# A column-tiled memory update, a second queue for the first input block, and a new set of scheduling priorities in a gated mix of memory attention and a gated feed-forward layer

## The chip, the cores and the metric

The kernel runs on one core of a Trainium2 chip. The metric is the device time of one execution in microseconds (us). All runs in this document are in the fast state: this is a program for one core, and no run was over 1.5% above the fastest of the same kernel. TensorE, VectorE, ScalarE and GpSimd are written PE, DVE, ACT and POOL in the profile; PEld is TensorE's weight load, and SP is the engine that issues most transfers.

## The reference

The output is `g*a + (1-g)*b`, where `a` is attention in four segments of 512 positions with a running memory, and `b` is a gated GELU layer. The part that matters here is the memory: after each segment `M` and `z` are updated from `phi(k)` and `v`, and the next segment reads them.

```python
x = A_x                                   # (1, 2048, 512) bf16; 32 heads of 16; N = 4 segments of L = 512
g = sigmoid((x * gate_w).sum(-1, keepdims=True))
phi = lambda t: where(t > 0, t + 1.0, exp(t))
for s in range(N):                        # q, k, v = x@wq, x@wk, x@wv, split by heads and segments
    p = softmax(qs @ ks.T * scale + mask)         # mask: causal inside the segment
    a_dot = p @ vs
    a_mem = (phi(qs) @ M) / (phi(qs) @ z + 1e-6)
    outs.append(gb * a_mem + (1 - gb) * a_dot)    # gb = sigmoid(beta), per head
    M = M + phi(ks).T @ vs                # the memory update: a 16 x 16 block per head
    z = z + phi(ks).sum(over positions)
a = concat(outs) @ wo
b = (gelu(x @ w_gate) * (x @ w_up)) @ w_down      # width 1792
# ... (reshapes, casts and the input generator are cut)
```

## The kernel before

The program is a graph of tasks. A list scheduler in the host code places them: at each step it takes the task that can start first by its estimates, and of several the one with the highest priority. A priority is the longest estimated path to the end plus a hand-tuned bias per task name. Thus the order of the instructions on every engine follows from the tasks, their estimates and the biases together.

```python
BIAS = {"D0": -56, "D1": -233, "D2": -96, ..., "mz0": -1, "mz1": -9, "mz2": -35, "mzacc0": 7, ...}   # some 130 entries
...
t.prio = min(t.est.values()) + best + t.bias      # best: the highest priority among the successors
...
k = (st, -t.prio - (OPEN_BONUS if open_ else 0.0), t.id)   # st: when the engine, the inputs and a PSUM bank are free
```

The memory update (tasks `mz`) of a segment multiplies `phi(k)`, four chunks `t` of 128 features (8 heads each), with the values of those heads and a column of ones, over four blocks `kt` of 128 positions. A matmul makes a 128 x 136 block, of which only the eight 16 x 17 blocks on the diagonal are wanted. VectorE adds the whole block to an accumulator (`mzacc`) and masks it (`mzbd`).

```python
for i in range(2):
    gm = Grp(banks)                       # one PSUM bank
    pieces(f"mz{s}_{i}", gm, [
        mm(gm, lambda gm=gm, t=t, i=i: gm.f32()[:, 136 * (t - 2 * i):136 * (t - 2 * i) + 136],
           phkt[:, kt, t * 128:(t + 1) * 128],
           Vaug[sl][:, kt, :, 4 * t:4 * t + 4, :].rearrange("p j i c -> p i j c"),
           [("phkt", t), ("Vaug", sl, kt)], kt == 0, kt == 3, 136)
        for t in (2 * i, 2 * i + 1) for kt in range(4)], 4)
    ...
    task(f"mzacc{s}_{i}", DVE, [first], grp=gm)          # copy or add of 272 columns
    task(f"mzbd{s}_{i}", DVE, [Instr(lambda e, i=i: e.tensor_tensor(
        MZbd[:, 2 * i:2 * i + 2, :], MZacc[:, 2 * i:2 * i + 2, :],
        bdmask[:, :].rearrange("p (o c) -> p o c", o=1).to_broadcast([P, 2, 136]), ALU.mult), ...)])
```

The product of probabilities and values (tasks `pv`, "PV" below) already works in column-tile mode: four matmuls, each with 17 weight columns in its own quarter of the array (`tile_position=(0, 32*q)`), run side by side: a group of four with 64 columns starts every 29 ns in the kernel before. The scores work in row-tile mode (32 contraction rows each). All else uses the full array.

At the start, the first block of x comes in two halves from the SP queue, then the weights. Sixteen transposes turn it, two into each of eight PSUM areas, and eight copies of 256 columns take it out. Six full-array matmuls on zeros run before that.

```python
for a in range(2):
    dma(f"x0_{a}", SP, lambda a=a: xin[:, 2 * a:2 * a + 2, :], ...)
for c0, c1 in ((0, 128), (128, 512)):
    for key, w, src in (("wk", wk, A_wk), ("wq", wq, A_wq)):
        wdma((key, c0 > 0), SP, ...)
...
for i in range(6):
    gw = Grp(banks)
    task(f"warm{i}", PE, [Instr(lambda e, gw=gw: e.matmul(gw.f32()[:, :], warm[:, 0:128], warm, ...)])
for u in range(2):                        # half of x
    for kb in range(4):                   # block of 128 features
        ...                               # two transposes into one area, one copy of 256 columns (ACT or DVE)
```

The softmax here doesn't subtract the row's maximum and nothing guards it: scores larger than these inputs give would overflow.

## Time and profile before

| What | Value |
|---|---|
| Time, median of the three runs there were | 272.45 us (272.41 to 272.8) |
| Span of the profiled execution | 270.3 us |
| DVE, ACT, POOL busy | 69%, 78%, 36% of the span |
| DMA, mean over the span | 61 GB/s |

The prediction below shows the page's lines on TensorE, so here are only two views that it tells in words. The first is the timeline of TensorE in the kernel before, at the start. A row has the start in us from the start of the span, the time until the last of the group ends, the engine, the source line, the operation, output and input, weight and moving sizes, the number of instructions, and in brackets how long the engine stood idle before it and what ended that.

```profile
3.80 1.06 PE L533 MATMUL psXALL<-ident,hT 128*128 128x128 bf16 x8
4.65 0.91 PE L533 MATMUL psW<-ident,hT 128*128 128x128 bf16 x8
5.71 1.02 PE L439 MATMUL psW<-xT,wk 128*128 128x512 bf16 x4
7.18 2.76 PE L439 MATMUL psW<-xT,wk 128*128 128x512 bf16 x12 [0.45 <-DMA wk<-in_A_wk_dram]
```

The sixteen transposes run into one another, the first K projection follows, and the other three wait 0.45 us for the second part of wk. The second view is the groups of the kernel before by instruction shape: busy time and mean ns after the first bar, idle time before them after the second.

```profile
L439 PE MATMUL psW<-vaug,phkt 128*128 128x136 bf16 x48 | 3.5, 224 | 0.0
L758 DVE TENSOR_TENSOR mzbd<-mzacc,bdmask 128x272 bf16<-128x272 f32 x6 | 2.5, 464 | 0.0
```

These are the 48 memory-update matmuls and the six masked products. 224 ns is the length of one record, not what a matmul costs: one starts every 63 ns, as the prediction works out.

### The profile page before, as it was taken

To read this page: it belongs to the slowest core of one execution; us is meant where nothing else is said; L and a number is where in the kernel's file an instruction comes from. 1 tells how busy PE (TensorE), PEld (TensorE's weight loads), DVE (VectorE), ACT (ScalarE), POOL (GpSimd) and SP (SyncE) were. 2 spreads that over 40 slices of the span, in tenths; PEclk is the share of its full clock that TensorE was granted. 3 is DMA by queue.
4 is the path that set the end of the run, shared out by engine and by line. 5 is a ranking of instruction groups with operands and counts; after the bars stand their busy time and mean duration, and the time that the engine had idled before them with its cause. 6 is when DMAs were issued, how large, how long until landed. Compare 5 with 4: busy or idle time off the path is not lost.

```text
span 270.3 us, 6945 instructions
## 1 busy us (share of the span) xinstructions
PE 260.6 (96%) x2928; PEld 122.1 (45%) x2969; DVE 186.9 (69%) x333; ACT 211.4 (78%) x180; POOL 96.5 (36%) x223
## 2 busy tenths in 40 slices
PE   7999999999999999999999999999999999999996
PEld 4444434345544353534444444534444444444454
DVE  2779888987889867878608969897642668443451
ACT  4998799989898897979778988986867767776602
POOL 8327785331003864432104723262200253352300
PEclk9999999999999999999999999999999999999999
DMA  6997992000213410032200320112020000000002
GB/s 192 208 308 157 372 230 24 0 4 2 41 39 65 104 49 23 2 78 41 44 0 0 41 42 19 41 23 62 19 44 0 1 2 2 19 22 23 18 2 78
DMA packets 32023, 16.52 MB, mean 61 GB/s; under 512 B 21368, under 2 KB 31992, under 8 KB 31992
## 3 DMA queue, kind: packets, MB, share of 16 engines
q1 hardware_dynamic: 31992, 16.07, 25.8%
q8 instruction: 23, 0.38, 0.6%
q14 instruction: 8, 0.07, 0.1%
HBM read 8.14 MB, written 2.10 MB: 38 GB/s over the span
## 4 chain that ended last, share of the span: by engine, by line
PE 89%; DVE 3%; ACT 3%; issue 2%; DMA 2%; SPq 1%; ACTq 0%
PE psW L439 72%; PE psXALL L774 8%; PE psW L823 5%; DMA wk<-in_A_wk_dram 2%; PE psXALL L439 1%; PE psW L831 1%; DVE oT L858 1%; ACT klow L638 1%; ACT pt L781 1%; ACT hT L908 1%; SPq L470 1%; DVE kpad_1 L661 0%; ACT L908 0%; DVE otok L725 0%; ACT pex L618 0%
## 5 line engine op out<-in xcount | busy, mean ns | idle before, releaser
L781 ACT ACTIVATE pt<-psXALL 128x2048 bf16<-128x2048 f32 x64 | 120.0, 1875 | 27.6 <-PE psXALL L774 22.9
L785 POOL TENSOR_SCALAR_AFFINE_SELECT pt<-pt 128x256 bf16<-128x256 bf16 x128 | 56.9, 446 | 142.8 <-ACT pt L781 121.1
L929 DVE TENSOR_TENSOR hT<-psW,hT 128x512 bf16<-128x512 f32 x56 | 37.8, 686 | 26.0 <-PE psW L439 25.6
L439 PE MATMUL psW<-xT,wu 128*128 128x512 bf16 x215 | 51.4, 380 | 1.3 <-issue 1.1
L439 PE MATMUL psW<-xT,wg 128*128 128x512 bf16 x214 | 49.7, 379 | 1.3 <-issue 1.0
L439 PE MATMUL psW<-wd,hT 128*128 128x512 bf16 x202 | 49.4, 380 | 0.9 <-issue 0.6
L838 DVE STREAM_TRANSPOSE tb<-psW 128x512 f32<-128x512 f32 x32 | 21.0, 696 | 19.1 <-PE psW L831 19.1
L439 PEld LDWEIGHTS psW<-xT,wg 128*128 128x128 bf16 x224 | 20.6, 98 | 25.3 <-issue 1.9
L439 PEld LDWEIGHTS psW<-xT,wu 128*128 128x128 bf16 x224 | 20.2, 98 | 24.5 <-issue 2.1
L439 PEld LDWEIGHTS psW<-wd,hT 128*128 128x128 bf16 x210 | 18.9, 98 | 22.9 <-issue 2.7
L908 ACT ACTIVATE hT<-psW 128x512 bf16<-128x512 f32 x28 | 16.5, 597 | 7.6 <-PE psW L439 7.6
L785 POOL TENSOR_SCALAR_AFFINE_SELECT ptl<-ptl 128x2048 bf16<-128x2048 bf16 x8 | 17.0, 2120 | 12.2 <-ACT ptl L781 10.2
L823 PE MATMUL psW<-pt,vaug 128*17 128x192 bf16 (+3 forms) x512 | 18.7, 273 | 0.0
L781 ACT ACTIVATE ptl<-psXALL 128x2048 bf16<-128x2048 f32 x8 | 15.0, 1877 | 4.6 <-PE psXALL L774 4.5
L439 PE MATMUL psW<-xT,wk 128*128 128x512 bf16 x60 | 15.2, 380 | 1.2 <-issue 0.6
L439 PE MATMUL psW<-xT,wq 128*128 128x512 bf16 x61 | 15.8, 379 | 0.3 <-issue 0.2
L693 POOL COPY exsT<-exs 32x4 f32<-32x4 f32 x64 | 14.5, 226 | 3.7
L439 PE MATMUL psW<-wo,oT 128*128 128x512 bf16 x56 | 14.9, 379 | 0.5 <-issue 0.5
L439 PE MATMUL psW<-wv,xT 128*128 128x512 bf16 x61 | 14.8, 380 | 0.3 <-issue 0.2
L981 DVE TENSOR_SCALAR ost<-psW,omgt 128x512 bf16<-128x512 f32 x8 | 6.0, 748 | 13.1 <-PE psW L439 13.1
L823 PEld LDWEIGHTS psW<-pt,vaug 128*17 128x17 bf16 x512 | 10.2, 90 | 8.2 <-POOL pt L785 2.1
L456 DVE CAST hT<-psW 128x512 bf16<-128x512 f32 x19 | 12.6, 678 | 0.9 <-PE psW L439 0.8
(104 smaller groups left out, 307.9 us busy)
## 6 DMA issues: line engine op xcount, KB each, us to landing
out_dram<-ost SPq DMA_DIRECT2D x15, 128.0 KB, 1.7
wg<-in_B_w_gate_dram SPq DMA_DIRECT2D x2, 896.0 KB, 6.7
wu<-in_B_w_up_dram SPq DMA_DIRECT2D x2, 896.0 KB, 6.0
wd<-in_B_w_down_dram SPq DMA_DIRECT2D x1, 1792.0 KB, 13.0
vlow<-vaug SPq DMA_DIRECT2D x8, 136.0 KB, 3.4
hT<-in_A_x_dram SPq DMA_DIRECT2D x2, 256.0 KB, 3.0
wv<-in_A_wv_dram SPq DMA_DIRECT2D x1, 512.0 KB, 6.3
wo<-in_A_wo_dram SPq DMA_DIRECT2D x1, 512.0 KB, 13.9
```

Source lines behind the costliest of these rows:

```text
L439: return Instr(lambda e: e.matmul(view(), lhsT, rhs, start=first, stop=last), reads=reads, writes=[fkey if fkey is not None else g.key], e ...
L456: alts[DVE] = [Instr(lambda e: e.tensor_copy(dst(), src()), reads=reads, writes=writes, est=dve_t(n))]
L470: return e.dma_start(out_ap(), in_ap())
L693: cross = task(f"exsT{s}", POOL, [Instr(lambda e, g=g, c=c: e.tensor_copy(exsT[sl][32 * g:32 * g + 32, c:16:4], exs[32 * c:32 * c + 32, s4 ...
L774: instrs.append(Instr(lambda e, g=g, lhs=lhs, rhs=rhs, c0=c0, ncol=ncol: e.matmul(X[g][:, c0:c0 + ncol], lhs(32 * g), rhs(32 * g), start=T ...
L781: prev_exp[0] = exp_task(s, f"exp{s}_{t}{name}", [Instr(lambda e: e.activation(dst[:], XALL[:, :].rearrange("p (g c) -> p g c", g=4), ACTF ...
L785: task(f"msk{s}_{t}{name}", POOL, [Instr(lambda e, view=view, pat=pat, base=base: e.affine_select(out=view, in_=view, compare_op=ALU.is_ge ...
L823: instrs.append(Instr(lambda e, t=t, q=q, kb=kb, slot=slot, c0=c0: e.matmul(gp.f32()[32 * q:32 * q + 17, 128 * kb + 64:512], Vaug[sl][:, k ...
L838: task(f"pvt{s}_{t}_{j}", DVE, [Instr(lambda e: e.transpose(Tb[:, j, :], gp.f32()[:, :]), [gp.key], [("Tb", j)], dve_t(512))], grp=gp)
L908: lambda e, g=g, ft=ft, s=s: e.activation(hT[s % 2][:, ft, :], g.f32()[:, :], ACTF.Gelu_apprx_tanh),
L929: task(f"Um{s}_{ft}", DVE, [Instr(lambda e, g=g, ft=ft: e.tensor_tensor(hT[sl][:, ft, :], g.f32()[:, :], hT[sl][:, ft, :], ALU.mult), [g.k ...
L981: DVE: [Instr(lambda e, view=view, gt=gt, tile=tile: e.tensor_scalar(ostage[tile % N_OST][:], view(), omgt[:, gt:gt + 1], None, ALU.mult), rd,
```

## The change

There are three parts. **Memory update:** each chunk of 128 features is cut in four tiles of 32 (two heads each), which run side by side in column-tile mode (25 to 33 ns for a group of four, as the traces below show), so that a tile makes 32 x 34 values instead of 128 x 136. This makes 64 small matmuls per segment instead of 16, one PSUM bank instead of two, and a quarter of the columns for TensorE to stream. The task carries the scheduler's tag of the PV bursts, so it can be placed inside one. **Start:** the second half of x0 is issued from the ACT queue, and the transposes are evacuated in four copies of 512 columns (two blocks of 128 features at a time, side by side in one PSUM bank) instead of eight of 256. **Priorities:** all biases are new. The code for a gate on VectorE is also added, but `GATE_DVE = ()` leaves it out of the program; that part of the diff is cut here, as are the buffers' declarations and the lines for the transposes.

```diff
 BIAS = {
-    "D0": -56, "D1": -233, "D2": -96, "D3": -332, "G0": -8, ...
+    "D0": -106, "D1": -371, "D2": -43, "G0": -115, ...
     (all entries replaced)
@@ start
-        dma(f"x0_{a}", SP, lambda a=a: xin[:, 2 * a:2 * a + 2, :],
+        dma(f"x0_{a}", (SP, ACT)[a], lambda a=a: xin[:, 2 * a:2 * a + 2, :],
 ...
-            dst = xT[0][:, kb, 256 * u:256 * u + 256]
+            dst = xT[0][:, 2 * i:2 * i + 2, 256 * u:256 * u + 256]
@@ memory update
-            for i in range(2):
-                gm = Grp(banks)
-                pieces(f"mz{s}_{i}", gm, [ ... 16 full-array matmuls, as above ...
+            gm = Grp(banks)
+            m = task(f"mz{s}", PE, [
+                Instr(lambda e, t=t, kt=kt, c=c: e.matmul(
+                    gm.f32()[32 * c:32 * c + 32, 34 * t:34 * t + 34].rearrange("p (j e) -> p j e", e=17),
+                    phkt[:, kt, t * 128 + 32 * c:t * 128 + 32 * c + 32], Vaug[sl][:, kt, :, 4 * t + c, :],
+                    start=(kt == 0), stop=(kt == 3), tile_position=(0, 32 * c)),
+                    [("phkt", t), ("Vaug", sl, kt)], [gm.key], 0.009)
+                for t in range(4) for kt in range(4) for c in range(4)], grp=gm)
+            m.tiled = "pv"
+            m.patience = PATIENCE
 ...
+            task(f"mzbd{s}", DVE, [ ... four products of 32 partitions x 136, instead of two of 128 x 272 ...
```

## The prediction

> **What bounds the kernel now.** I read the page first (parts 1, 2 and 4).
>
> ```profile
> PE 260.6 (96%) x2928; PEld 122.1 (45%) x2969; DVE 186.9 (69%) x333; ACT 211.4 (78%) x180; POOL 96.5 (36%) x223
> PE   7999999999999999999999999999999999999996
> PEclk9999999999999999999999999999999999999999
> PE 89%; DVE 3%; ACT 3%; issue 2%; DMA 2%; SPq 1%; ACTq 0%
> ```
>
> TensorE is busy 96% of 270.3 us at full clock, in every slice but the first and the last, and 89% of the chain that ended last is TensorE. Busy time alone does not prove a bound, because matmul records overlap, so I then read start-to-start times off the timeline of TensorE:
>
> ```profile
> 53.58 0.40 PE L774 MATMUL psXALL<-qT,kpad_0 32*128 32x320 bf16 x8
> 53.90 0.61 PE L823 MATMUL psW<-pt,vaug 128*17 128x448 bf16 x16
> 54.34 0.29 PE L831 MATMUL psW<-ptl,vlow 128*17 128x64 bf16 x16
> 54.46 0.61 PE L823 MATMUL psW<-pt,vaug 128*17 128x448 bf16 x16
> 54.90 0.29 PE L831 MATMUL psW<-ptl,vlow 128*17 128x64 bf16 x16
> 55.34 0.81 PE L439 MATMUL psW<-xT,wg 128*128 128x512 bf16 x3 [0.16 <-issue]
> ...
> 64.89 0.81 PE L439 MATMUL psW<-wv,xT 128*128 128x512 bf16 x3
> 65.53 1.17 PE L439 MATMUL psW<-vaug,phkt 128*128 128x136 bf16 x16
> 66.54 0.59 PE L439 MATMUL psW<-xT,wq 128*128 128x512 bf16 x2
> ```
>
> From these: two 512-column matmuls end 0.59 us after the first starts and one lasts 0.38, so one starts every 0.21 us (0.216 in the single records). Sixteen memory-update matmuls take (1.17 - 0.22)/15 = 63 ns each. In column-tile mode (L823, L831) four matmuls run at a time: the sixteen of L831 start at 54.34 and the next group at 54.46, so a group of four 64-column ones costs (54.46 - 54.34)/4 = 0.03 us (29 ns in single records). I then compared every stretch of the weight-load records, which are complete (2969), with these pitches plus one cost per change of mode. From about 7.2 us on the whole execution leaves only about 3 us unexplained, spread over some 160 stretches, none above 0.3 us. So between 7.2 us and the last matmul (267.7) TensorE is issue-bound without real gaps: what is taken off TensorE's issue time comes off the span, and work of other engines is hidden. The beginning is the one place where it waits:
>
> ```profile
> 2.33 4.80 DMA wk<-in_A_wk_dram
> 7.18 1.05 PE psW L439 x4
> ```
>
> The second K projection starts when the second part of wk lands (7.13 us).
>
> [...] the step from a 512-column matmul to a row-tile one is 0.312 us in place of 0.216, so about 0.095 us; row-tile to column-tile costs about the same (0.171 after a 192-column group that itself needs 0.077). [...] This trace has column tiles only with 17-column weights; the change loads 32, so no record of it tells the cost. [...] (216 ns at 512 columns; the one-column gate matmuls start every 25 ns). [...] the first two x0 issues are 0.51 us apart and land 0.75 us apart (3.70 and 4.45).
>
> **The change part by part.**
>
> Memory update, the main part. Removed: 3 segments x 16 matmuls x 63 ns = 3.02 us of TensorE. Added: 3 x 64 matmuls with 34 columns and 32-column weights, four at a time, 16 groups per segment. [...] I take it to start no faster than the floor of 25 to 29 ns; at 27 ns a segment is 0.43 us, three are 1.30 us. Gain 1.72 us. Modes: the order in which instructions stand in the two built programs shows segments 1 and 2 between score matmuls and a PV burst, which had a change of mode there already. Segment 0 stands between score matmuls and gate matmuls, which costs one more row-to-column change: 164 changes before, 165 after, +0.09 us. Net -1.63 us. All other matmuls are the same in number and shape, so TensorE's remaining issue time is the same.
>
> Evacuation of the memory: VectorE loses six copies or adds (414 to 431 ns) and six masked products (464), about 5.3 us, and gets three additions of 136 columns (about 0.3) and twelve 32-partition products (about 0.25): about 4 us. At 69% busy this is hidden.
>
> Start. The second x0 half is issued at about 0.8 us on ACT instead of 1.33 on SP, and all weight loads move up by 0.5 us. But the trace shows the stretch from about 3 to 7 us as a chain of landings (3.70, 4.45, 5.57, 7.13) for 256, 256, 128 and 384 KB, that is, limited by transfer, not by issue: the same bytes come before wk's second part. Also the 16 transposes start every 0.107 us [...] from 3.80 to 5.5, with no gap at the arrival of the second half, so this half is not awaited now; and if both halves share the engines, the first may land later. Evacuation in four instructions of 512 columns (about 0.6 on ACT, from the 595 ns row of the same size, and 0.43 on VectorE) instead of eight of 256 (0.38 and 0.29) saves perhaps 0.2 us of engine time but starts the last one later. I expect wk's second part 0.0 to 0.5 us earlier and TensorE able to use about half of it: -0.2 us.
>
> New priorities. They reorder nearly all rows: all V projections of segment 0 now come before the first scores, so the first exponentials start some 3.5 us later, and memory update 0 moves from 65 us to near 27. They can remove no TensorE work, and before there was nearly nothing to win from gaps (about 3 us of small change). The risk is one-sided: ACT has 22% idle, but a new place where scores wait for an exponential or PV for its mask would show. I allow +0.2 us. The tail (24 matmuls of 512 and 36 of 256 after the last PV) is the same in both orders.
>
> Sum: 272.45 - 1.63 - 0.2 + 0.2 = 270.8; because some of the small change may go with fewer stretches I say 270.7.
>
> **The rivals.** (a) Weight loads become the limit of the tiled memory update. [...] gain only 0.5 us, time about 271.9. For it: [...] 192 more load and matmul pairs than the 48 removed. Against it: the 17-column groups run at the pace of their streams. One in four. (b) The instructions themselves limit: 128 tiny ones in a row, then 128 of PV. The PV bursts run 128 in 1.1 us without a wait; 32 klow pairs ran in 0.23 us, so bursts are fast, but none this long was tested. It would give about the same loss. One in eight. (c) The new order starves TensorE: 3.5 us of later exponentials come back as a wait at the turn of a segment, where ACT must finish all exponentials before the gelus. It would make 271.5 to 273. One in eight. (d) The start gains in full: 0.5 us or more, time 270.2 or less. One in five. (e) VectorE or a DMA becomes the bound: no, VectorE loses work and the DMA is idle most of the time.
>
> **Range and chances.** Best case: all of the mz gain at 20 ns per group (2.0 us) and 0.6 us at the start and 0.4 of small change: 269.4. Worst likely: weight loads limit and 1 us of new stalls: 272.4. Two per cent is 5.45 us: even deleting the whole memory update, 3.0 us, would not reach it, and a loss of 5.45 us needs gaps that this scheduler did not leave before. So nearly all chance is on the same.
>
> **What would show it.** The memory-update group: 192 matmuls with 64 in about 0.6 us (0.43 plus the 0.2 us a last record lasts); rival (a) or (b) if 64 take over 0.9. The landing of wk's second part and the first start after it: earlier than 7.18 by 0 to 0.5. Idle time of TensorE between 8 us and the end: as small as now; rival (c) if the waits of scores on ACT grow by a microsecond. The prediction is wrong if the span falls by more than 3.0 us (work I have not seen went away, or gaps I took for fixed costs) or rises.

## The result, and the profile after

The changed kernel took 270.35 us in the median (270.18 to 272.21, six runs), the kernel before 272.38 us in the same rounds (271.75 to 272.8, six runs). The ratio of the fast runs is 0.9936 with an interval of 0.9909 to 0.9963, which is "the same" at 2%. A ratio is here always the mean time of one kernel's fast runs over that of the other's of the same rounds, so it is not quite the ratio of the medians quoted. The six times after are 270.18, 270.26, 270.29, 270.40, 270.43 and 272.21; the profile happens to be of the last, which is an outlier that has to be explained on its own.

These are the lines on busy time and on the chain's engines of the page of the changed kernel.

```profile
PE 266.1 (98%) x3113; PEld 121.6 (45%) x3113; DVE 186.0 (69%) x333; ACT 212.1 (78%) x179; POOL 95.2 (35%) x223
PE 97%; DMA 1%; ACT 0%; issue 0%; ACTq 0%
```

There are 144 more weight loads (2969 before), which is 192 less 48, and the chain is now nearly all TensorE: VectorE and ScalarE, 3% each before, are gone from it. The busy time of TensorE is higher than before, but that count is not complete: 41 of 2969 matmul records were missing before (2928) and none after. The weight-load records are complete in both, and all start-to-start times below are from them.

The timeline of TensorE in the changed kernel shows the memory update of segments 0 and 1 in their places (segment 2 is shown with an experiment).

```profile
27.21 0.40 PE L788 MATMUL psXALL<-qT,kpad 32*128 32x448 bf16 x8
27.54 0.72 PE L755 MATMUL psW<-vaug,phkt 128*32 128x34 bf16 x64
28.19 0.60 PE L442 MATMUL psW<-xT,wg 128*128 128x512 bf16 x2
...
100.23 0.71 PE L755 MATMUL psW<-vaug,phkt 128*32 128x34 bf16 x64
100.82 0.62 PE L837 MATMUL psW<-pt,vaug 128*17 128x448 bf16 x16
101.26 0.30 PE L845 MATMUL psW<-ptl,vlow 128*17 128x64 bf16 x16
101.51 0.62 PE L837 MATMUL psW<-pt,vaug 128*17 128x448 bf16 x16
```

The 64 matmuls are one uninterrupted group of about 0.7 us with its tail, where sixteen full ones took 1.17. From the first load of the update to the first load of what follows it is 0.648 us in segment 0, with the change back to full mode in it, 0.564 us in segment 1 and 0.545 us in segment 2. In segment 1, the second PV group starts 0.25 us after the L845 group before it, where the same step is 0.12 in the PV bursts that the prediction shows: it waits for VectorE's addition of the memory update. This view of the changed kernel, the instructions that touch `mzacc`, shows that addition (columns after the count: shortest, median, longest ns; the time of the first and of the last).

```profile
L770 DVE TENSOR_TENSOR mzbd<-mzacc,bdmask x12: 279/290/297, 31.3 to 163.1; 32x136 bf16<-32x136 f32 x12
L767 DVE TENSOR_TENSOR mzacc<-psW,mzacc x2: 299/300/301, 101.1 to 161.7; 128x136 f32<-128x136 f32 x2
```

The addition runs from 101.1 to 101.4, and the PV group follows at 101.51. In segment 2 the same step is 0.11 us, so this is the only place where the new update adds a wait. Now the start, first from the chain of the changed kernel, then from its timeline.

```profile
0.81 3.40 DMA hT<-in_A_x_dram
4.26 1.48 PE psXALL L536 x12
5.75 0.61 ACT xT L543
6.41 12.28 PE psW L442 x48
```

```profile
6.41 5.37 PE L442 MATMUL psW<-xT,wk 128*128 128x512 bf16 x16 [0.26 <-ACT xT L543]
```

Before, the second K projection waited for wk. In this execution the chain goes through x0: its landing, the transposes, one evacuation on ScalarE. All 16 K matmuls then follow without a break, but in this execution they took 5.37 us, and the single records show one start every 427 ns until about 10.1 us, twice the usual 216: TensorE was still at half its usual pace. (This is read from the steps, and the recorded expectations call it the half clock; the granted clock in the profile stands at 1.00 throughout.) This is what makes it the slow one of the six.

### The profile page after: what moved, and what is told of

Same layout as the page of the kernel before. It is cut to its first block, busy times and chain, and to the rows that moved or that the text cites. A ratio compares the mean times of both kernels' runs of the same rounds, so it can differ in the third digit from the quotient of the medians.

```text
span 270.5 us, 7272 instructions
## 1 busy us (share of the span) xinstructions
PE 266.1 (98%) x3113; PEld 121.6 (45%) x3113; DVE 186.0 (69%) x333; ACT 212.1 (78%) x179; POOL 95.2 (35%) x223
## 4 chain that ended last, share of the span: by engine, by line
PE 97%; DMA 1%; ACT 0%; issue 0%; ACTq 0%
PE psW L442 78%; PE psXALL L788 9%; PE psW L837 6%; PE psXALL L442 1%; PE psW L845 1%; DMA hT<-in_A_x_dram 1%; PE psW L755 1%; PE psXALL L536 1%; ACT xT L543 0%; ACT ost L971 0%; ACTq L337 0%
## 5 line engine op out<-in xcount | busy, mean ns | idle before, releaser
L799 POOL TENSOR_SCALAR_AFFINE_SELECT pt<-pt 128x256 bf16<-128x256 bf16 x128 | 55.4, 434 | 139.3 <-ACT pt L795 132.7
L442 PE MATMUL psW<-xT,wu 128*128 128x512 bf16 x224 | 52.7, 380 | 0.0
L442 PE MATMUL psW<-xT,wg 128*128 128x512 bf16 x224 | 52.3, 380 | 0.0
L442 PE MATMUL psW<-wd,hT 128*128 128x512 bf16 x210 | 51.7, 380 | 0.0
L788 PE MATMUL psXALL<-qT,kpad 32*128 32x320 bf16 (+3 forms) x512 | 25.5, 273 | 0.0
L788 PEld LDWEIGHTS psXALL<-qT,kpad 32*128 32x128 bf16 x512 | 7.6, 92 | 26.5 <-ACT pt L795 20.8
L442 PE MATMUL psW<-xT,wk 128*128 128x512 bf16 x64 | 17.2, 412 | 0.3 <-ACT xT L543 0.3
L442 PE MATMUL psW<-wo,oT 128*128 128x512 bf16 x60 | 15.8, 381 | 0.0
L459 DVE CAST hT<-psW 128x512 bf16<-128x512 f32 x21 | 14.1, 680 | 1.7 <-PE psW L442 1.5
```

The lines of the kernel that those rows point to most:

```text
L442: return Instr(lambda e: e.matmul(view(), lhsT, rhs, start=first, stop=last), reads=reads, writes=[fkey if fkey is not None else g.key], e ...
L459: alts[DVE] = [Instr(lambda e: e.tensor_copy(dst(), src()), reads=reads, writes=writes, est=dve_t(n))]
L788: instrs.append(Instr(lambda e, g=g, lhs=lhs, rhs=rhs, c0=c0, ncol=ncol: e.matmul(X[g][:, c0:c0 + ncol], lhs(32 * g), rhs(32 * g), start=T ...
L799: task(f"msk{s}_{t}{name}", POOL, [Instr(lambda e, view=view, pat=pat, base=base: e.affine_select(out=view, in_=view, compare_op=ALU.is_ge ...
```

## The experiments

Eleven kernels were run, in three calls; kernels of one call share the runs of the kernel before, on the same chip. To compare traces without the randomness of the start, I use one length throughout: from the first weight load after the 16 loaded for the K projections to the last weight load of the execution. I call it the body; the time up to it is the start. All traces have some 3.0 us after the last load, but for mz_only with 3.75.

### after_again: the changed kernel once more

Nothing is edited. It gives a profile of a typical execution and the comparison for the other runs of its call.

> The changed kernel once more, unchanged, for a profile of a typical execution. Theory: the profiled execution of 272.21 us was slow because its K projections ran at half clock (427 ns from start to start until 10.1 us); a typical one has 216 ns there, a span near 268.6 us and a time near 270.3 us, 2.0 us less than the kernel before. Rival: the half clock belongs to the change and this profile shows it again, with a time near 272. In either case the memory update takes 0.55 to 0.60 us per segment.

The median is 270.32 us (269.78 to 270.60, five runs) against 272.11 (271.55 to 272.56, 27 runs); ratio 0.9936 [0.9924, 0.9947]. The result repeats. The start in the timeline of TensorE:

```profile
4.17 1.89 PE L536 MATMUL psXALL<-ident,hT 128*128 128x128 bf16 x16 [0.17 <-DMA hT<-in_A_x_dram]
6.32 3.84 PE L442 MATMUL psW<-xT,wk 128*128 128x512 bf16 x16 [0.26 <-ACT xT L543]
```

The K matmuls take 3.84 us here instead of 5.37. The body starts at 9.78 us instead of 11.40, and is 256.10 us long against 256.09: the outlier lost its time before the body and nowhere else. The kernel before has a body of 257.70 us that starts at 9.57. So the change takes **1.60 us off the body**, exactly alike in two executions.

### mz_full: the new order with full-array memory updates

On every engine the order of the changed kernel is kept; only the matmuls of the task `mz` are the old ones. The result is wrong on purpose: to fit one bank, the blocks of 136 columns overlap and the evacuation reads wrong columns (relative error 0.39). What is issued does not depend on the values, and the granted clock is 0.999 to 1.0 in both.

```diff
-    ... 64 matmuls of 32 weight columns x 34, estimate 0.009 each
+    Instr(lambda e, t=t, kt=kt: e.matmul(
+        gm.f32()[:, (0, 136, 272, 376)[t]:(0, 136, 272, 376)[t] + 136], phkt[:, kt, t * 128:(t + 1) * 128],
+        Vaug[sl][:, kt, :, 4 * t:4 * t + 4, :].rearrange("p j i c -> p i j c"),
+        start=(kt == 0), stop=(kt == 3)), ..., 0.036)
+    for t in range(4) for kt in range(4)
```

> The changed kernel in its own order on every engine, but each tiled memory update replaced in place by 16 full-array matmuls of 136 columns (the result is wrong on purpose, one block overlaps another in PSUM). Theory: 16 x 63 ns = 1.01 us in place of 0.57 us in three places, and one change of mode more in sum (one fewer in segment 0, one more in segments 1 and 2): +1.3 us from the matmuls and +0.1 us, so 1.4 us slower than the changed kernel. Rival: the gain came from the start and the priorities: less than 0.5 us slower.

The median is 271.61 us (271.22 to 272.23, 21 runs), ratio 0.9983 [0.9977, 0.9989]. Against the changed kernel in the same call, the tiled form is worth 271.61 - 270.32 = **1.29 us**; the bodies say 257.37 - 256.10 = 1.27 us. Segment 2 in the timelines, first of mz_full, then of after_again:

```profile
160.05 1.18 PE L755 MATMUL psW<-vaug,phkt 128*128 128x136 bf16 x16
161.16 0.62 PE L837 MATMUL psW<-pt,vaug 128*17 128x448 bf16 x16
```

```profile
159.37 0.67 PE L755 MATMUL psW<-vaug,phkt 128*32 128x34 bf16 x64
159.94 0.61 PE L837 MATMUL psW<-pt,vaug 128*17 128x448 bf16 x16
```

From the update to the PV group after it is 1.11 us in the one and 0.57 in the other. In the body the new order with the old matmuls is 257.70 - 257.37 = 0.33 us shorter than the kernel before. It does so although the full-array update stands between tiled groups in it, with 166 changes of mode against 164; at the 0.095 us of the prediction this costs 0.19 us, so the new order removes about 0.5 us of waits. That the tiled form gives the larger part is shown by this run; the 0.5 us is worked out, and no run has that order with nothing else changed.

### mz_twice: every memory-update matmul issued twice

```diff
-                for t in range(4) for kt in range(4) for c in range(4)], grp=gm)        # estimate 0.009
+                for _ in range(2) for t in range(4) for kt in range(4) for c in range(4)], grp=gm)   # 0.0045
```

The order stays the same, and so does the result, as the second pass starts its accumulation anew.

> The changed kernel with every tiled memory-update matmul issued twice (same result, the same order elsewhere). Theory: the first 32 pairs of load and matmul of a burst start at 25 ns per group of four and the rest are limited by the rate at which TensorE is fed, about 11.8 ns per pair: the 64 added pairs per segment cost 64 x 11.8 = 0.76 us, three are +2.3 us. Rival: the pace of the array, 25 to 27 ns per group: 3 x 16 x 27 = +1.3 us.

The bursts of 128 take 1.180, 1.097 and 1.079 us where those of 64 took 0.646, 0.563 and 0.543: 64 more pairs of load and matmul cost 0.53 us, **8.3 ns a pair or 33 ns for a group of four**, not the 27 of the prediction. The single records show where the rate changes. These are the starts of every eighth pair in segment 1, in ns after the first:

| Pair | 0 | 8 | 16 | 24 | 32 | 40 | 48 | 56 | 64 | 96 | 120 |
|---|---|---|---|---|---|---|---|---|---|---|---|
| after_again (64 pairs) | 0 | 43 | 93 | 143 | 220 | 287 | 379 | 446 | 563 (PV) | | |
| mz_twice (128 pairs) | 0 | 43 | 93 | 143 | 220 | 286 | 353 | 420 | 486 | 753 | 979 |

For the first 31 pairs eight take 50 ns, that is 25 ns for a group of four; from then on eight take 66 or 67 ns, but for single steps of 34 ns (before pair 32 in both, before pair 48 in after_again). The 25 ns are the step from one group of four tiles to the next; inside a group the loads start 1 to 6 ns apart. My reading was that the first pairs are queued beforehand and the rest are fed at one pair per 8.3 ns; this was not shown. Pair 32 is also one of those that carry a semaphore wait, as pairs 16 and 48 do. So the two rates and the place of the break are measured; their cause is open.

The time was a miss: 274.73 us (273.40 to 275.51, six runs), ratio 1.0093 [1.0072, 1.0114], 4.4 us over the changed kernel, where 2.3 were expected and the longer bursts explain 1.6. The timeline of mz_twice in segments 1 and 2 shows what else was lost.

```profile
99.64 0.58 PE L837 MATMUL psW<-pt,vaug 128*17 128x448 bf16 x10
101.05 0.28 PE L837 MATMUL psW<-pt,vaug 128*17 128x192 bf16 x6 [0.82 <-issue]
...
160.82 1.21 PE L755 MATMUL psW<-vaug,phkt 128*32 128x34 bf16 x128
161.93 0.61 PE L837 MATMUL psW<-pt,vaug 128*17 128x448 bf16 x16
...
163.68 0.39 PE L788 MATMUL psXALL<-qT,kpad 32*128 32x320 bf16 x6
164.64 0.26 PE L788 MATMUL psXALL<-qT,kpad 32*128 32x192 bf16 x2 [0.57 <-issue]
```

Inside one PV group TensorE stands still, with no semaphore that it waits for ("issue"), after 138 pairs from the start of the burst: no load starts for 1.20 us. In segment 2 the same happens in the scores after the PV burst, for 0.94 us. The longer bursts and the two standstills, less the steps that would stand there anyway, come to some 3.6 us, about the 3.4 us by which the body of this execution is longer (259.53 us). The profiled run was the fastest of the six (273.40), so the others lost more. A block of 16,384 bytes of instructions moved on the instruction queue from 98.86 to 99.82 us, just before the first gap, and another from 162.28 to 163.25, 0.45 us before the second, so late arrival of instructions would fit; nothing here proves it, and I leave it open. What it does show is that a long burst of tiny matmuls can cost far more than its rate (here 4.4 us where the longer bursts explain 1.6).

### mz_wide: twice the columns in each matmul

The moving operand is repeated, so a matmul streams 68 columns instead of 34; the evacuation reads the first 34 of each 68, and the result is correct.

```diff
-    ... Vaug[sl][:, kt, :, 4 * t + c, :],
+    ... Vaug[sl][:, kt, :, 4 * t + c, :].rearrange("p (o j) e -> p o j e", o=1).to_broadcast([P, 2, 2, 17]),
```

> The changed kernel with the moving operand of the memory update doubled to 68 columns by a repeat (the second half is not used; same result, same number of instructions). Feeding theory: the burst is limited by the number of instructions, so 0.57 us per segment grows by at most 0.1 us, +0.0 to +0.3 us in sum. Rival, the time goes by columns: 34 more columns are 14 ns in 16 groups of 3 segments, +0.7 us.

The median is 270.47 us (270.04 to 270.85, five runs), ratio 0.9944 [0.9932, 0.9956]; the body is 256.14 us against 256.10, and the bursts 0.665, 0.574 and 0.563 us. Only the first part is slower (after the first eight pairs, eight take 62 to 70 ns there instead of 50), and the 8.3 ns a pair begin later, at pair 48, in segment 2 not at all. So doubling the pairs costs 8.3 ns for each, and doubling the columns next to nothing: the update costs what its **number of pairs** costs. Its columns do not set the pace, nor does a load of 32 columns as such, since half the starts are at 25 ns a group with four such loads each. No run separates the two instructions of a pair.

### mz_mixed: the update dealt out among the matmuls of a PV burst

If a feed rate limits, tiny pairs placed between longer ones should start at 25 ns a group again. After the scheduler, the 64 pairs of segments 1 and 2 were cut in four parts of 16, and one part was put after each of the four long groups of the PV burst that follows.

```diff
+            mz, pv, ins_list = taken[t].alts[PE], ins_list, []
+            for i in range(4):
+                ins_list += pv[4 * i:4 * i + 4] + mz[16 * i:16 * i + 16]
+            ins_list += pv[16:]
```

> The changed kernel with the memory updates of segments 1 and 2 cut in four and put between the four long groups of the PV burst that follows them (the same tile mode, same result; segment 0 as it was). Doubling the update cost 0.53 us per 64 added pairs, 8.3 ns per pair, so 64 pairs alone last 0.55 us [...]. Feeding theory: beside the long streams of PV the pairs are fed in time, so update and first PV burst last [...] 0.82 us in place of 1.10, and the 0.15 us by which the PV burst of segment 1 was late goes too: 0.5 to 0.7 us faster than the changed kernel. Rival, each pair has a price of its own wherever it stands: within 0.2 us of it.

It failed: 270.85 us (270.53 to 271.08, seven runs), ratio 0.9935 [0.9909, 0.9960] in its call; the body is 256.66 us, 0.56 longer than that of the changed kernel. The timeline of mz_mixed in segment 1 shows why.

```profile
99.19 0.34 PE L755 MATMUL psW<-vaug,phkt 128*32 128x34 bf16 x16
99.43 0.29 PE L845 MATMUL psW<-ptl,vlow 128*17 128x64 bf16 x16
...
100.12 0.61 PE L837 MATMUL psW<-pt,vaug 128*17 128x448 bf16 x16 [0.39 <-DVE mzacc L767]
```

The first three parts did run at 25 ns a group, each after one pause of 0.07 to 0.18 us; the fourth ran at 8.3 ns a pair again. But the update and the first long PV matmuls together were no shorter for it: up to the first load of L845 they took 0.96 us in segment 1 and 1.01 us in segment 2, against 1.00 and 0.98 in after_again, where 0.82 was expected (an estimate: 0.55 us for the PV burst, and 16 groups of 34 columns at some 17 ns, as the line through the measured 29 ns at 64 columns and 216 ns at 512 gives). So this run does not support the feeding theory. Above all, in segment 1 the last part now ends just before the second PV group, which needs the bank that VectorE's addition still reads: from the L845 group to that PV group it is 0.69 us (0.39 of it idle) instead of 0.25, of which 0.12 is there without a wait. In segment 2 the update and the PV burst took 1.88 us together instead of 1.79. Putting the update ahead of the PV burst, as the changed kernel does, gives its evacuation a PV group of time to hide in.

### x0_sp_frozen: the second half of x0 issued from SP again

The order of all else is kept; the transfer alone goes back to the SP queue.

```diff
-            em.plan(t.eng, ins)
+            em.plan(SP if t.name == "x0_1" else t.eng, ins)
```

> The changed kernel in its own order, only the second half of x0 issued from SP again, so wk, wq and wv are issued 0.5 us later. Theory: wk's second part lands near 7.1 us as in the kernel before, in place of 6.4 to 6.7; the first transposes start near 3.75 in place of 4.1 to 4.25. The second K projection starts at 7.15 to 7.2, where the changed kernel shows 6.6 to 7.7 [...]; the time within 0.3 us of the changed kernel. Rival, the issue from ACT is worth its 0.5 us: 0.5 us slower.

The median is 270.59 us (270.18 to 270.84, six runs), ratio 0.9923 [0.9895, 0.9951]. No cost can be seen, as the interval holds the 0.9936 of the changed kernel; but it is 1.5 us wide, so it does not exclude the rival's 0.5 us either. The timeline of TensorE in x0_sp_frozen:

```profile
3.79 1.91 PE L536 MATMUL psXALL<-ident,hT 128*128 128x128 bf16 x16
5.97 4.14 PE L442 MATMUL psW<-xT,wk 128*128 128x512 bf16 x16 [0.26 <-ACT xT L543]
```

The landings are 3.57 and 4.30 us for the halves and 7.08 for the second part of wk. In the nine profiled executions with both queues they are 4.04 to 4.27, 4.37 to 4.51, and 6.27 to 7.18. So issuing from ACT mostly brings wk forward, by up to 0.8 us, but makes the first half late by about half a microsecond (3.55 to 3.74 us over the traces with one queue); the second half, issued half a microsecond earlier, lands no earlier (4.26 to 4.45 with one queue). In two executions the effects cancel: the body starts at 9.73 us here and at 9.78 in after_again. They do not always: the fifth K matmul, the first that needs the second part of wk, starts at 7.14 here, and with both queues at 6.56 in mz_twice, where TensorE sped up early (its transposes took 1.04 us from first to last instead of 1.47), and at 7.22 in mz_mixed, where wk landed at 7.18 and was waited for.

### evac_split: each paired evacuation cut in two

```diff
-  ACT: [Instr(lambda e, dst=dst, src=src: e.activation(dst, src, ACTF.Copy), [key], wr, act_t(512))],
+  ACT: [Instr(lambda e, ..., k=k: e.activation(dst[:, k, :], src[:, k, :], ACTF.Copy), [key], [wr[k]], act_t(512) / 2)
+        for k in range(2)],      # the same for DVE; engines and order unchanged
```

> The changed kernel in its own order, only each of the four paired evacuations of x0 as two of 256 columns again, on the same engines. Theory: two of 256 cost 0.77 us on ACT in place of 0.60 and 0.58 on VectorE in place of 0.43; the last of them lies on the path to the first K projection, so that starts 0.1 to 0.2 us later; the time 0.0 to 0.2 us more.

The median is 270.32 us (269.94 to 270.85, six runs), ratio 0.9914 [0.9886, 0.9943]; body 256.09 us, which starts at 9.42. Within what the runs can tell, pairing the copies is worth nothing.

### warm7: one more matmul on zeros ahead of the transposes

```diff
-    for i in range(6):
+    for i in range(7):
```

In the slow execution that was profiled the K matmuls start 427 ns apart until 10.1 us. If that came from a warm-up that is just too short, a longer one should help; if the moment at which the steps shorten to 216 ns has another cause, it should not.

> The changed kernel with seven warm-up matmuls in place of six, which fill the gap between the last warm-up and the first transpose (3.8 to 4.25 us). Theory: the half clock in the profiled execution, 427 ns per matmul until 10.1 us, comes from this gap; [...] none lies 1.5 us above the others, and the median falls by 0 to 0.4 us. Rival, [...] the same median and spread as the changed kernel.

The median is 270.77 us (269.91 to 272.81, 16 runs), ratio 0.9939 [0.9921, 0.9957]. One of 16 runs was again 2 us slow, and the spread of the others is not smaller. The body is 256.09 us. The moment at which the steps shorten differs between the traces: the K matmuls of the outlier were at 427 ns until 10.1 us, while in the profiles of mz_twice and mz_wide the transposes, 107 ns apart in the outlier and in the kernel before, already sped up (1.04 and 1.11 us from first to last instead of 1.47). The kernel before has such outliers too (274.08 and 274.30 among 22 runs of that call). What sets the moment was not found.

### mz_only, prio_only and start_only: each part by itself

Each is the kernel before with one part of the change: the new memory update, the new biases, or the two edits of the start. The scheduler then makes its own order.

```diff
 mz_only:     kernel before + the memory-update part of the diff
 prio_only:   kernel before, BIAS = { ... the new table ... }
 start_only:  kernel before + the start part of the diff
```

> The kernel before with the tiled memory update alone (its evacuation too), old start and old priorities; the list scheduler makes a new order. Theory: TensorE's issue time falls by the 1.3 us that the full-array update cost more in the changed kernel, the start stays at 7.17 us for the second K projection, so 0.8 to 1.4 us faster than the kernel before, less what the new order adds in waits. Rival, the tiled update pays only with the new priorities: within 0.4 us of the kernel before.

> The kernel before with the new priorities alone. Theory: priorities take no work off TensorE; in the kernel before only some 0.5 us of waits were there to win (0.19 us at 16 us and 0.27 us at 179 us), and these priorities were made for another set of tasks: between 0.4 us faster and 0.8 us slower. Rival, the priorities carry the gain: over 0.8 us faster.

> The kernel before with the new start alone (second half of x0 from ACT, evacuation in pairs), old memory update and old priorities. Theory: wk's second part lands at 6.3 to 6.7 us and the second K projection starts at 6.6 to 7.7, [...] in place of 7.17: on the median 0.0 to 0.4 us faster, with a wider spread. Rival, the start carries the gain: over 0.8 us faster.

All three missed, and all three are slower than the kernel before (272.25 us, 271.92 to 272.46, 11 runs):

| Kernel | Median us (range, runs) | Ratio to before | Body us |
|---|---|---|---|
| mz_only | 300.77 (300.22 to 303.20, 6) | 1.1064 [1.1035, 1.1092] | 285.46 |
| prio_only | 273.82 (273.06 to 275.13, 6) | 1.0060 [1.0041, 1.0079] | 258.98 |
| start_only | 275.73 (275.33 to 277.51, 5) | 1.0146 [1.0123, 1.0169] | 261.26 |

The extreme case is the most telling. These are the slices of TensorE and its clock on the page of mz_only (40 equal slices of 7.5 us), and its longest waits (total us, times, longest us):

```profile
PE   7999799999999999955479999997899999999995
PEclk9999999999999999986577999999799999999999
```

```profile
PEld psXALL L773 <- ACT pt L780: 35.3, 48, 2.9
PE psXALL L773 <- ACT pt L780: 14.4, 10, 2.6
```

and for comparison the first of these waits in after_again, with the same columns:

```profile
PEld psXALL L788 <- ACT pt L795: 22.9, 54, 0.4
```

Then the windows from 120 to 160 us, of mz_only and of after_again. The columns are the window, its length, busy time and count of TensorE, weight loads, DVE, ACT and POOL, the granted clock, the DMA share and GB/s.

```profile
120.00:140.00 20.00, 14.39 (x225) 6.78 (x222) 13.62 (x24) 8.31 (x5) 3.65 (x8) 0.83 0.04 8
140.00:160.00 20.00, 11.68 (x136) 3.93 (x136) 8.72 (x12) 15.85 (x11) 7.16 (x13) 0.66 0.00 1
```

```profile
120.00:140.00 20.00, 19.58 (x242) 9.32 (x246) 11.80 (x21) 15.85 (x18) 4.14 (x10) 1.00 0.14 29
140.00:160.00 20.00, 19.73 (x230) 9.15 (x235) 14.68 (x25) 17.47 (x18) 9.69 (x25) 1.00 0.21 40
```

With the old biases and the new task set, the scheduler puts groups of scores next to each other with few or no other matmuls between; each then waits for ScalarE to finish an exponential, up to 2.9 us instead of 0.4, and TensorE loses part of its clock as well (0.66). The removal of TensorE work turned into a wait 20 times its size. In start_only the same happens in small: steps of 1.35 us between starts, where TensorE waits for the exponential of the low blocks, and of 1.65 us, where it waits for a copy of q. In prio_only there is one of 1.04 us, with a wait for `mzbd`; besides, in its profiled execution the two parts of wk landed at 6.68 and 7.93 us instead of 5.57 and 7.13, and the body started at 10.37 us, 0.80 later than before. Why they landed late is not on record. The three effects, +28.5, +1.6 and +3.5 us, do not add up to -1.8: the new biases fit the new tasks, and only those. A part of this change cannot be priced by adding it alone to the old kernel; keeping the order frozen, as mz_full and x0_sp_frozen do, prices it.

## Why the prediction was right

The prediction was 270.7 us with a range of 269.4 to 272.4; the medians are 270.35 and, repeated, 270.32. Its steps fared less evenly than the sum. The measured column is in the terms of the prediction.

| Step | Predicted us | Measured us | From |
|---|---|---|---|
| TensorE bound: work taken off it comes off the span | yes | 1.27 in the trace, 1.29 in the time | mz_full |
| 48 full-array matmuls removed | -3.02 | the same pitch of 63 ns was used | before |
| 48 groups of four added | +1.30 | +1.66 (0.55 + 0.56 + 0.54) | burst lengths, segment 0 less one change of mode |
| A wait added by the update | 0 | +0.14 | PV group at 101.51 |
| One more change of mode | +0.09 | +0.09 (165 against 164) | counted, size as predicted |
| Order, priorities and small change | +0.1 | about -0.5 | what is left of the body's -1.60 |
| Start | -0.2 | about -0.2, random by far more | what is left of the time's -1.8 |

**The bound.** Right. With the order held, the three bursts up to the next load are together 1.43 us shorter than in mz_full; less the added wait of 0.14 us that is 1.3, and the time is 1.29 us shorter; the chain became 97% TensorE.

**The memory update.** The mechanism was right, the size off. The step that failed is "I take it to start no faster than the floor of 25 to 29 ns; at 27 ns a segment is 0.43 us". The 25 ns are there, but only for the first half; the other half costs 33 ns a group, and a segment takes 0.55 us. This comes nearest to the prediction's rival (b), "the instructions themselves limit", at 0.3 to 0.4 of the size given to it (0.36 us, or 0.50 with the added wait, of the 1.2 between the gains of 1.72 and 0.5), though why pairs cost 8.3 ns is open. Rival (a), weight loads as the limit, does not hold for the first half, where four loads of 32 columns start every 25 ns; for the second half no run separates load and matmul. The claim "all other matmuls are the same ... TensorE's remaining issue time is the same" missed the PSUM bank that the PV group waits for in segment 1.

**The evacuation.** Right: hidden, but for that one wait. The twelve products took 279 to 297 ns each, not 250.

**The priorities.** The step "the risk is one-sided" and "there was nearly nothing to win from gaps" was wrong in sign: the new order took about 0.5 us of the 3 us of small change, net 0.33 us with the full-array update in its place; this is worked out from mz_full, not measured by itself. Two errors of about 0.5 us, this one and the memory update, cancelled by luck. That is why the sum is better than its terms.

**The start.** The size cannot be told from chance: the 0.2 us is what is left over, and executions differ by more. The mechanism held in part. "I expect wk's second part 0.0 to 0.5 us earlier and TensorE able to use about half of it": with this start it landed at 6.27 to 7.18 us, against 7.13 before, and undoing the second queue showed no cost that the runs resolve. In most executions the start is now paced by the x0 chain and by the pace at which TensorE runs through it (K matmuls 216 or 427 ns apart); the body starts at 9.15 to 9.78 us in the typical executions with this start, at 9.57 before, and at 11.40 in the slow one. That the first half might land later was foreseen, and it did, by about half a microsecond. The executions that are 2 us slow were not foreseen, and their cause is open.

**The rivals (c) to (e).** The order did not starve TensorE in this kernel, though with one part alone it did so by up to 28.5 us. The start did not gain 0.5 us. No other engine became the bound.

## What to carry to other kernels

When TensorE has no gaps, cutting the area of a matmul into tiles pays by the time between starts, and for tiles this small that went by the number of pairs of load and matmul here (8.3 ns for each added pair, next to nothing for twice the columns): count pairs, not columns. A list scheduler's order belongs to one set of tasks and estimates, so judge an edit with the order frozen, and tune the priorities anew with every change of the tasks. A start that hangs on a transfer, an evacuation and the pace of TensorE at once is worth timing over many runs before a gain of 0.2 us is believed.
